# Attention and MLP-Mixer kernel on one core: laying older channel MLP steps between the token MLP's steps by their length

## The chip, the core and the metric

One core of one Trainium2 chip runs the whole program. The metric is the device time of one execution in microseconds (us). Times are told as the median of several runs, and one further execution is recorded by the hardware profiler; positions such as "at 455.01" are microseconds from the start of that recording's span.

TensorE (PE) multiplies into PSUM, of which this kernel gives each kind of product a few buffers. VectorE (DVE), ScalarE (ACT) and GpSimd (POOL) do the rest. SyncE (SP) issues most DMAs, ScalarE most loads of q and k. The program gives every engine its instructions in one fixed order.

## The reference

```python
scores = matmul(q, k.T) / 8                       # 8 batch rows, 8 heads, 576 tokens, 64 wide
scores = where(scores >= max(scores) - tau, scores, -1e9)
attn   = softmax(scores)
x      = (attn @ v) as (8, 576, 512)              # heads side by side
u      = x + (relu(x^T @ w_tok1) @ w_tok2)^T      # token MLP: 576 -> 256 -> 576
out    = u + relu(u @ w_ch1) @ w_ch2              # channel MLP: 512 -> 1536 -> 512
```

All of it is in 32-bit floats.

## The kernel before, in words

The kernel has one stream for attention and one for the two MLPs, and lays both into one order per engine by hand.

**Attention in units.** There are 144 units, 18 for each batch row b; unit u holds 128 query rows of a pair of heads. `scores(u)` (L290) makes the products `sc` on PE (L304), their maxima `mx` on VectorE (L309) and `bias` on GpSimd (L310). `weigh(u)` (L313) is ScalarE's: the threshold as a Prelu (L319, two instructions, which also set the two `sc` buffers free) and the exponential (L326, two). `norm` (L330) scales the result. Two units later `turn_blocks` (L359) turns it on VectorE (L367, tile `T`), and after every third unit 16 DMAs on SyncE's queue (L376) carry `T` into `eT`. I call these 16 an eT batch; there is one buffer for it. Two units after that, `values` (L393) multiplies `eT` by v on PE (tile `pv`, L411 and L416), and ScalarE copies the result to `xT` (L421).

**The token MLP.** When a row's last `values` is done, `push(b)` (L579) puts the row's token MLP in the list `todo`: five transposes `tx` (L447, each copied to `x_sb` by ScalarE, L448), two products `tok1` (L454, each with a Relu into `a` on ScalarE, L456), and eight products `tok2` (L464, each added to `xT` by VectorE, L468). The first `tok1` needs all five copies, the first `tok2` both Relus, and `xT` is what the channel MLP reads. So there are places where each step depends on the one just before it.

**The channel MLP.** Two batch rows are 1152 tokens, in groups i = 0 to 4 of 256 (the last of 128). Groups 0 and 1 come after the even row's token MLP, groups 2 to 4 after the odd one's. A group is 12 steps `ch1` (L501; four products each, L507, then a Relu on ScalarE, L508) and, for each 128 tokens, the steps `ch2` (L515; 12 products in all, L528, three to a step, then an addition or copy on VectorE, L540 or L546, and the output's DMA, L547). A product of 32-bit floats is two matmul instructions, so a `ch2` step of three products is six. From the second pair of rows on, `ch1(1)` also starts a turn of `xT` on VectorE (L491) and 16 DMAs on SyncE's queue (tile `ut`, L497), which are issued from `move_u` (L553). `tok1`, `tok2`, `ch1` and `ch2` share two PSUM buffers, tag `mm`; one `ch2` tile holds its buffer through all its steps.

**How the MLP's steps come into the order.** Each step in `todo` has an estimated cost in us. `push` sets a `quota` for each unit, such that some 45 us of steps (20 in the first row) are still left when the next row's token MLP arrives. In each unit `fill` (L566) takes steps until a share of the quota is used: 0.4 of it after the scores, before `weigh`, and three times 0.2 between the instructions of `weigh` (L322 to L328). The share in which a step falls decides where its ScalarE instruction stands: a Relu of the first share stands ahead of that unit's Prelus, one of the later shares behind them.

The steps left over (`old`) are the cover for the token MLP: `push` lays them between its steps (L588 to L591).

```python
for i, step in enumerate(steps):
    n = 2 if i in waits else 1
    todo.extend(old[:n] + [step])
    del old[:n]
```

Here `waits` holds two indices: that of the first `tok1` and that of the first `tok2`. So one old step stands ahead of each token step and two ahead of these, whatever the old steps' lengths are (`ch2` 2.6, `ch1` 1.72, in the group of 128 tokens 0.86). In this program `push(1)` finds 2 old steps of 2.6, the later rows find 19 to 23 steps of together 36 to 41.

Of the kernel before, what the change touches and what calls it, by code (L numbers as in the profile page):

```python
# [21 lines left out]
def kernel(  # L22
# [39 lines left out]
    NJ = DCH // P  # L62
# [162 lines left out]
    def weight(n):  # L225

        nonlocal steps_done
        for k in range(steps_done, min(steps_done + n, 3 * len(pieces) + 1)):
            i, part = divmod(k, 3)
            if part == 0:  # L230
                on_gpsimd(i - 1)
                if i:
                    load_piece(i - 1 + NRAW)
            else:
                on_scalar(i + 1, part - 1)
            on_vector(i, part)
            steps_done = k + 1
# [5 lines left out]
    def need(i):  # L243

        weight(3 * i + 4 - steps_done)
# [236 lines left out]
    def channel_mlp(b, uT, i):  # L482

        s = {}
        n = min(GR, 2 * S - GR * i)
        nt = n // P

        def turn_u():

            us, ut = s["us"], s["ut"]  # L490
            nc.vector.transpose(  # L491
                out=us[:, 0:nt].rearrange("q n a (c d) -> q c (n a) d", c=NCC),
                in_=uT[:, :, GR * i : GR * i + n].rearrange("q c (m r) -> q c m r", r=32),
            )

            def move(a, k):
                nc.sync.dma_start(out=ut[32 * a : 32 * a + 32, 0:nt, k, :], in_=us[32 * k : 32 * k + 32, 0:nt, a, :])  # L497

            moves.extend([lambda a=a, k=k: move(a, k) for a in range(4) for k in range(4)])

        def ch1(j):  # L501
            need(7 + j)
            if j == 0:
                s["g"] = work.tile([P, NJ, GR], F32, tag="g", bufs=1, name=f"g_{b}_{i}")
            ps = ps_mm.tile([P, GR], F32, tag="mm", name=f"c1_{b}_{i}_{j}")[:, 0:n]
            for c in range(NCC):
                nc.tensor.matmul(ps, lhsT=wc1[:, j, c, :], rhs=uT[:, c, GR * i : GR * i + n], start=(c == 0), stop=(c == NCC - 1))  # L507
            nc.scalar.activation(out=s["g"][:, j, 0:n], in_=ps, func=AF.Relu)  # L508
            if j == 1:
                s["us"] = work.tile([P, GR // P, 4, NCC * 32], F32, tag="us", bufs=1, name=f"us_{b}_{i}")  # L510
                if b:
                    s["ut"] = work.tile([P, GR // P, 4, NCC * 32], F32, tag="ut", bufs=1, name=f"ut_{b}_{i}")
                    turn_u()

        def ch2(t, part):  # L515
            need(7 + NJ + 3 * part + 2)
            t0 = GR * i + P * t
            if part == 0:
                s["ps"] = ps_mm.tile([P, NCC, P], F32, tag="mm", name=f"c2_{b}_{i}_{t}")
            ps = s["ps"]  # L520
            flat = ps.rearrange("q c d -> q (c d)")
            if part == 0 and not b:
                for c in range(NCC):
                    nc.tensor.matmul(
                        ps[:, c, :], lhsT=uT[:, c, t0 : t0 + P], rhs=ident, is_transpose=True, start=(c == 0), stop=False, skip_group_check=True
                    )
            for j in range(3 * part, 3 * part + 3):
                nc.tensor.matmul(  # L528
                    flat,
                    lhsT=s["g"][:, j, P * t : P * t + P],  # L530
                    rhs=wc2[:, j, :],
                    start=(j == 0 and b > 0),
                    stop=(j == NJ - 1),
                    skip_group_check=True,
                )
            if part == 3:
                o = s["us"][:, t].rearrange("q a x -> q (a x)")
                if b:
                    move_u()
                    nc.vector.tensor_add(  # L540
                        out=o.rearrange("q (c k d) -> q c k d", c=NCC, k=4),
                        in0=ps.rearrange("q c (k d) -> q c k d", k=4),
                        in1=s["ut"][:, t].rearrange("q k (c d) -> q c k d", c=NCC),
                    )
                else:
                    nc.vector.tensor_copy(out=o, in_=flat)  # L546
                nc.sync.dma_start(out=out[b : b + 2].rearrange("b s d -> (b s) d")[t0 : t0 + P, :], in_=o)  # L547

        return [(0.0067 * n, lambda j=j: ch1(j)) for j in range(NJ)] + [
            (2.6 if part or b else 3.0, lambda t=t, part=part: ch2(t, part)) for t in range(nt) for part in range(4)  # L550
        ]

    def move_u():  # L553
        while moves:
            moves.popleft()()
# [6 lines left out]
    todo = deque()  # L562
# [16 lines left out]
    def push(b):  # L579
        nonlocal quota  # L580
        uT = xTs[b]
        steps, waits = token_mlp(b) if b else token_mlp(b, range(NP // 2, NP))
        old = list(todo)
        todo.clear()
        todo.extend(early)
        early.clear()

        for i, step in enumerate(steps):  # L588
            n = 2 if i in waits else 1
            todo.extend(old[:n] + [step])  # L590
            del old[:n]  # L591
        todo.extend(old)
        for i in range(2) if b % 2 == 0 else range(2, (2 * S + GR - 1) // GR):
            todo.extend(channel_mlp(b - b % 2, uT, i))
        quota = (sum(c for c, _ in todo) - (KEEP if b else KEEP_FIRST)) / (UB - 1)
# [6 lines left out]
    def values_due(u):  # L602
        while due and due[0][0] <= u:
            _, b, p0, g = due.popleft()
            values(b, p0, g)
            if b == 0 and p0 == 0 and g == 2:
                return True
            if p0 == NP - 2 and g == 2:
                if not in_blocks(b):
                    return True  # L610
                push(b)
        return False

    for u in range(len(units) + LAG + 4):
# [4 lines left out]
        if on:  # L619
            b_now, p0, t = units[u]  # L620
            n = b_now * NP + p0
# [24 lines left out]
        if last and u < UB:  # L646
            early.extend(token_mlp(0, range(NP // 2))[0])
        elif last:
            push(0)
# [79 lines left out]
```

## Time and profile before

| | |
|---|---|
| median of 5 runs | 1353.02 us (1351.87 to 1355.48) |
| the profiled execution's own time | 1351.55 us |
| its span in the profile | 1349.8 us, 1.75 less than its time |
| mean granted clock of TensorE | 0.993 |
| `ch2` products (L528), 128x512 | 864 matmuls, 389.5 us busy |
| `ch1` products (L507) | 1920 matmuls, 399.6 us busy |
| `sc` products (L304) | 1280 matmuls, 192.9 us busy |
| eT batches (L376) | 672 DMAs, 108.0 KB each, median 2.3 us from issue to landing |

How to read it: the profile's "busy" of PE is a union of overlapping instructions, since matmuls are pipelined. What a product really takes is the distance from its start to the next one's start. In this profile that is 0.43 us for a matmul of 512 columns, 0.24 for `tok2`'s 288, 0.21 for 256 and 0.11 for 128, with hardly any spread; a longer distance is a wait. The first part of the run (to about 200 us) is short of MLP work and is not touched by the change.

### The profile page before, as it was taken

How to read it: one execution, taken by the hardware profiler on the slowest of the kernel's cores; microseconds unless marked ns; L12 is line 12 of the kernel's file. 1: busy time of each engine (PE TensorE's matmuls, PEld its weight loads, DVE VectorE, ACT ScalarE, POOL GpSimd, SP SyncE). 2: the span in 40 equal slices, each digit the busy share in tenths (PEclk: the TensorE clock that was granted, in tenths of full speed). 3: DMA queues.
4: the chain of work that ended last, by engine and by line, in shares of the span. 5: the costliest groups of instructions: out<-in, count | busy, mean ns of one | idle time of the engine just before them, and what ended most of it. 6: DMA issues, size and time to landing. Idle time of an engine off the chain costs nothing.

```text
span 1349.8 us, 17794 instructions
## 1 busy us (share of the span) xinstructions
PE 1303.3 (97%) x6138; PEld 808.8 (60%) x6138; DVE 592.6 (44%) x1024; ACT 585.3 (43%) x1299; POOL 353.6 (26%) x683
## 2 busy tenths in 40 slices
PE   6888899999999999999999999999999999999998
PEld 4555656547474666655665567565656566575675
DVE  6888874445443434444334445434433454201000
ACT  6777754445454435443434445353333444120110
POOL 4566652222222213221212222222221222100000
PEclk8998999999999999999999999999999999999999
DMA  5434774535353544543345435435443453400000
GB/s 123 118 90 124 203 174 95 129 93 131 91 136 80 119 103 100 128 103 90 85 110 128 95 88 126 116 82 119 106 103 84 118 112 82 115 16 18 22 24 32
DMA packets 296538, 135.31 MB, mean 100 GB/s; under 512 B 204736, under 2 KB 289216, under 8 KB 296448
## 3 DMA queue, kind: packets, MB, share of 16 engines
q1 hardware_dynamic: 167840, 118.15, 34.4%
q10 hardware_dynamic: 128608, 16.01, 7.5%
q8 instruction: 49, 0.80, 0.3%
q14 instruction: 41, 0.34, 0.1%
HBM read 43.25 MB, written 9.44 MB: 39 GB/s over the span
## 4 chain that ended last, share of the span: by engine, by line
PE 85%; DVE 6%; DMA 3%; ACT 2%; SPq 2%; POOL 1%; issue 1%; ACTq 0%; DVEq 0%; POOLq 0%
PE c L528 27%; PE c L507 25%; PE sc L304 11%; PE pv L416 8%; PE t L454 5%; PE t L464 4%; PE pv L411 3%; DVE mx L309 2%; SPq L376 2%; PE tx L447 1%; ACT e L319 1%; DMA eT<-T 1%; DMA lq<-in_q_dram 1%; DMA lk<-in_k_dram 1%; PE tr L355 1%
## 5 line engine op out<-in xcount | busy, mean ns | idle before, releaser
L309 DVE TENSOR_REDUCE mx<-sc 128x1 f32<-128x576 f32 x288 | 204.3, 750 | 445.9 <-PE sc L304 445.9
L507 PE MATMUL c<-xT,wc 128*128 128x256 f32 (+1 forms) x1920 | 399.6, 362 | 0.3 <-ACT g L508 0.3
L528 PE MATMUL c<-wc,g 128*128 128x512 f32 x864 | 389.5, 597 | 0.0
L507 PEld LDWEIGHTS c<-xT,wc 128*128 128x128 f32 x1920 | 334.4, 191 | 69.2 <-issue 29.3
L310 POOL TENSOR_SCALAR bias<-mx,toff 128x1 f32<-128x1 f32 x288 | 82.2, 285 | 774.2 <-DVE mx L309 719.2
L319 ACT ACTIVATE e<-sc,bias 128x576 f32<-128x576 f32 x288 | 199.2, 739 | 178.0 <-POOL bias L310 175.2
L528 PEld LDWEIGHTS c<-wc,g 128*128 128x128 f32 x864 | 159.2, 190 | 181.3 <-issue 177.9
L326 ACT ACTIVATE e<-e,ntau 128x576 f32<-128x576 f32 x288 | 221.1, 771 | 0.0
L337 POOL TENSOR_SCALAR e<-e,rr 128x576 f32<-128x576 f32 x288 | 214.4, 756 | 14.6 <-ACT g L508 2.6
L508 ACT ACTIVATE g<-c 128x256 f32<-128x256 f32 (+1 forms) x240 | 86.7, 361 | 294.1 <-PE c L507 275.9
L304 PE MATMUL sc<-kT,qT 64*128 64x288 f32 (+1 forms) x1280 | 192.9, 433 | 13.2 <-DVE kT L286 7.1
L367 DVE STREAM_TRANSPOSE T<-e 128x1152 f32<-128x1152 f32 x126 | 171.9, 1365 | 5.5 <-DMA eT<-T 3.5
L304 PEld LDWEIGHTS sc<-kT,qT 64*128 64x128 f32 (+1 forms) x1280 | 106.7, 178 | 99.7 <-issue 56.5
L416 PE MATMUL pv<-eT,lv 128*64 128x384 f32 (+1 forms) x1024 | 136.4, 406 | 0.0
L416 PEld LDWEIGHTS pv<-eT,lv 128*64 128x64 f32 x1024 | 76.3, 137 | 48.8 <-issue 40.1
L421 ACT COPY xT<-pv 128x384 f32<-128x384 f32 (+1 forms) x56 | 20.9, 400 | 165.9 <-PE pv L416 162.2
L540 DVE TENSOR_TENSOR us<-c,ut 128x512 f32<-128x512 f32 x27 | 18.6, 690 | 155.0 <-PE c L528 139.4
L464 PE MATMUL t<-w,a 128*128 128x288 f32 x256 | 75.2, 421 | 8.1 <-DVE xT L468 4.7
L454 PE MATMUL t<-x_sb,w 128*128 128x512 f32 (+1 forms) x180 | 72.4, 549 | 0.0
L464 PEld LDWEIGHTS t<-w,a 128*128 128x128 f32 x256 | 45.9, 192 | 30.1 <-issue 10.5
L468 DVE TENSOR_TENSOR xT<-xT,t 128x288 f32<-128x288 f32 x64 | 28.3, 446 | 71.0 <-PE t L464 70.5
L326 ACT ACTIVATION_READ_ACCUMULATOR e<-e,ntau 128x1 f32 x288 | 56.7, 197 | 0.0
(46 smaller groups left out, 542.9 us busy)
## 6 DMA issues: line engine op xcount, KB each, us to landing
eT<-T SPq DMA_DIRECT2D x672, 108.0 KB, 2.3
scratch<-in_moe_w_ch_dram SPq DMA_DIRECT2D x24, 512.0 KB, 3.7
lv<-in_v_dram SPq DMA_DIRECT2D x32, 288.0 KB, 3.2
out_dram<-us SPq DMA_DIRECT2D x36, 256.0 KB, 2.2
lk<-in_k_dram ACTq DMA_DIRECT2D x111, 72.0 KB, 2.6
lq<-in_q_dram ACTq DMA_DIRECT2D x106, 72.0 KB, 2.3
ut<-us SPq DMA_DIRECT2D x192, 32.0 KB, 1.9
lq<-in_q_dram SPq DMA_DIRECT2D x22, 72.0 KB, 3.3
```

Source lines behind the costliest of these rows:

```text
L304: nc.tensor.matmul(sc[h][rows, f, 0:HS], lhsT=qT[r, cols], rhs=kT[r, HS * f : HS * f + HS], start=True, stop=True)
L309: nc.vector.tensor_reduce(out=mx[:, c], in_=sc[h][:, :, 0:HS], axis=AX.XY, op=ALU.max)
L319: nc.scalar.activation(out=eh, in_=sc[h][:, :, 0:HS], func=AF.Prelu, bias=bias[:, h : h + 1], scale=SCALE, alpha=STEEP)
L326: nc.scalar.activation(out=eh, in_=eh, func=AF.Exp, bias=ntau, accum_out=rs[:, h : h + 1])
L337: nc.gpsimd.tensor_scalar(out=eh, in0=eh, scalar1=rr[:, h : h + 1], scalar2=1.0, op0=ALU.mult, op1=ALU.mult)
L367: nc.vector.transpose(out=T[:, :, place, :].rearrange("p a (c x) -> p c a x", c=NK), in_=e.rearrange("p (c a x) -> p c a x", c=NK, a=4))
L416: nc.tensor.matmul(to[r], lhsT=lv[:, j, :], rhs=e[j], start=False, stop=(c == NI - 1), skip_group_check=True)
L454: nc.tensor.matmul(to, lhsT=w1[:, t, P * m : P * m + P], rhs=x_sb[:, t, cols], start=(t == 0), stop=(t == NT - 1))
L464: nc.tensor.matmul(to, lhsT=a[:, m, P * c : P * c + P], rhs=w2[:, m, HS * f : HS * f + HS], start=(m == 0), stop=(m == NTK - 1))
L507: nc.tensor.matmul(ps, lhsT=wc1[:, j, c, :], rhs=uT[:, c, GR * i : GR * i + n], start=(c == 0), stop=(c == NCC - 1))
L508: nc.scalar.activation(out=s["g"][:, j, 0:n], in_=ps, func=AF.Relu)
L528: nc.tensor.matmul(flat, lhsT=s["g"][:, j, P * t : P * t + P], rhs=wc2[:, j, :], start=(j == 0 and b > 0), stop=(j == NJ - 1), skip_group_ ...
```

## The change

```diff
 def channel_mlp(b, uT, i):
+    J = 1 if b == 0 and i == 1 else 3
...
-        def ch2(t, part):
-            need(7 + NJ + 3 * part + 2)
+        def ch2(t, part, J):
+            need(7 + NJ + J * part + J - 1)
...
-            for j in range(3 * part, 3 * part + 3):
+            for j in range(J * part, J * part + J):
...
-            if part == 3:
+            if J * part + J == NJ:
...
-            (2.6 if part or b else 3.0, lambda t=t, part=part: ch2(t, part)) for t in range(nt) for part in range(4)
+            (0.867 * J + (0.0 if part or b else 0.4), lambda t=t, part=part: ch2(t, part, J)) for t in range(nt) for part in range(NJ // J)
         ]
...
     def push(b):
...
         for i, step in enumerate(steps):
-            n = 2 if i in waits else 1
-            todo.extend(old[:n] + [step])
-            del old[:n]
+            room = (3.4 if b == 1 else 5.0) if i in waits else 0.1
+            while old and room > 0:
+                room -= old[0][0]
+                todo.append(old.pop(0))
+            todo.append(step)
         todo.extend(old)
```

Ahead of a token step there is still one old step (a room of 0.1 is used up by any step). Ahead of the two steps in `waits` there are now as many as it takes to fill 5.0 us (3.4 for row 1). The `ch2` steps of group 1 of the first pair of rows, which are what `push(1)` finds, are cut to one product each, that is to two matmul instructions. The cost of a `ch2` step of three becomes 2.601 where it was 2.6. No instruction is added or removed: the change moves PE's steps, with the ScalarE, VectorE and SyncE instructions that belong to them, past the units' own instructions.

## Prediction, made before the changed kernel was run

> **What bounds the kernel now.** I read the busy shares first, then PE's waits, then the order of time around each of them, and at last the DMA queue of SyncE.
>
> ```profile
> PE 1303.3 (97%) x6138; PEld 808.8 (60%) x6138; DVE 592.6 (44%) x1024; ACT 585.3 (43%) x1299; POOL 353.6 (26%) x683
> ```
>
> PE is the bound, and the change neither adds nor removes one of its instructions. It can win only waits of PE, and lose only by new ones. PE's waits between 250 and 1180 us (engine, line, who was waited for: total us, times, longest) are few:
>
> ```profile
> PE t L464 <- ACT g L508: 3.2, 3, 1.6
> PE t L464 <- DVE xT L468: 1.8, 2, 1.3
> PE tx L447 <- ACT x_sb L448: 1.5, 2, 1.2
> PE pv L411 <- DMA lq<-in_q_dram: 0.5, 1, 0.5
> PE pv L411 <- DMA eT<-T: 0.3, 1, 0.3
> ```
>
> About 7 us, half of it the wait that the change aims at. Below I count from start to start, which gives 0.1 to 0.2 more for each. The releaser of the first is telling: not the Relu of `tok1` (L456) but one of `ch1` (L508). Around it, in unit 63:
>
> ```profile
> 450.21 1.24 PE L304 MATMUL sc<-kT,qT 64*128 64x288 f32 x8
> 451.38 2.05 PE L507 MATMUL c<-xT,wc 128*128 128x128 f32 x16
> 455.01 1.24 PE L464 MATMUL t<-w,a 128*128 128x288 f32 x4 [1.58 <-ACT g L508]
> ```
>
> Two short `ch1` fill both `mm` buffers. Their Relus stand behind the unit's Prelus on ScalarE, which wait for maxima and bias (452.63 to 454.04). The third user of a buffer waits, whoever it is.
>
> **A bound that is not in that list.** `values` needs its eT batch. From the turn `T` (L367) to the last landing it takes 12 to 15 us, and how much PE work lies between is set by the order. I took for each batch the landing (last issue plus some 2.3 us) and the start of `values`; the difference is its slack. From 200 us on it is under 1.2 us in twelve of 38 batches, and at the end of unit 36 PE waits already:
>
> ```profile
> 246.91 0.55 PE L411 MATMUL pv<-eT,vl 128*64 128x192 f32 x4 [1.70 <-DMA lq<-in_q_dram]
> ```
>
> (The load named is not what it waits for: in the built program this instruction waits for the batch, whose last DMA was issued by 244.0.) So each order that does less PE work between `T` and `values` pays there.
>
> **The change part by part.** I compared the orders in which the two built programs give PE its instructions, and counted at each unit and each `values` by how much more or less of the MLP stands ahead of it (0.86 us for a `ch2` product, 1.72 for a `ch1`, 0.86 for a short one, 0.97 for a `tok2`).
>
> *What goes.* (a) Row 1: seven single products now stand ahead of the transposes, one each, two ahead of `tok1`. The transposes waited 0.4 and 1.4 for ScalarE's copies (280.48, 282.38); with 0.86 between them, I find each copy (0.57) done in time: **-1.8**. (b) The first `tok2` waits 1.74, 0.99 and 0.99 in rows 2, 4, 6 (455.0, 770.4, 1086.9); as it comes later these go: **-3.7**. (c) Small waits of 0.24, three times, in row 4's `tok2` (779 to 794): -0.7. (d) `values` at 429.5 and 1088.3, which wait 0.3 and 0.4: -0.7. Together -6.9.
>
> *What takes its place on PE.* In row 2, unit 63, four short `ch1` stand where two stood. The third now needs the first one's buffer: ready at 454.04 + 0.26 = 454.3, wanted at 451.38 + 2 x 0.9 = 453.2, so 1.1, and 0.1 for the fourth: **+1.2**. In rows 4 and 6 the old steps go ahead of `tok1` so far that the first `tok1` slips behind the scores of units 98 and 134, into the first share of `fill`: its Relu then stands ahead of those units' Prelus, and the next scores, which need these buffers, wait. Before has this in unit 79, with a `ch1` of 1.72 as cover (order of time, all engines):
>
> ```profile
> 591.88 1.89 PE L507 MATMUL c<-xT,wc 128*128 128x256 f32 x8
> 592.08 0.60 ACT L456 ACTIVATE a<-t 128x512 f32<-128x512 f32 x1 [5.17 <-PE t L454]
> 592.57 1.36 ACT L319 ACTIVATE e<-sc,bias 128x576 f32<-128x576 f32 x2
> 593.70 1.53 PE L304 MATMUL sc<-kT,qT 64*128 64x288 f32 x8
> ```
>
> There the scores take 1.53 where others take 1.24: 0.3 lost. In units 98 and 134 the cover is 0.87, so 0.3 + 0.85, less what the first of the two buffers allows: 1.0 each, **+2.0** (bounds 0.3 and 1.2). Row 5 gets unit 79's pattern once, +0.3. In rows 4 and 6 no old step is left behind the last `tok2`: `ch1(0)` needs its buffer, which VectorE's addition frees some 2.2 after the scores' end (from 297.51 to 299.24 in unit 43, plus 0.45), while two `tok2` cover 1.94: 0.3 each, +0.7. Two or three `tok2` waits of the kind (c) arise in rows 2 and 6: +0.6. The `values` at 1088.3 still wait 0.3, with 0.1 of work put off: +0.4.
>
> *What the shifted order does to the batches.* (1) `values` of 246.9: one product (0.86) less ahead, batch unmoved, PE waits already: **+0.9**. (2) A whole `ch2` step (2.57) moves ahead of unit 52, so `T` comes 2.57 later against the work, and `values` at 383.71 stands where it stood:
>
> ```profile
> 363.25 1.24 PE L304 MATMUL sc<-kT,qT 64*128 64x288 f32 x8
> 364.42 5.42 PE L528 MATMUL c<-wc,g 128*128 128x512 f32 x12
> 369.77 1.24 PE L304 MATMUL sc<-kT,qT 64*128 64x288 f32 x8
> ...
> 383.71 0.55 PE L411 MATMUL pv<-eT,vl 128*64 128x192 f32 x4
> ```
>
> ```profile
> 367.57 13.47 SPq L376 DMA_DIRECT2D eT<-T  x16
> ```
>
> The batch ends at 381.04, its last DMA was issued 0.6 before and lands at 382.8: slack 0.9. Wait 2.57 - 0.9 = **+1.7** (0 if the batch shrinks to its shortest span, 10.3). (3) Unit 67 gets 2.57 more and a `tok2` (0.97) less ahead of it: 1.6 later, and its `T` 0.4 later still behind that `tok2`'s addition. From here SyncE's queue runs without a pause up to `values` at 530.56, which waits 0.45 already:
>
> ```profile
> 489.19 13.16 SPq L376 DMA_DIRECT2D eT<-T  x16
> 502.46 0.53 SPq L547 DMA_DIRECT2D out_dram<-us  x1
> 506.03 10.18 SPq L497 DMA_DIRECT2D ut<-us  x16
> 516.32 11.73 SPq L376 DMA_DIRECT2D eT<-T  x16
> ```
>
> (The gap at 503 is the output's landing, which VectorE's turn of `us` waits for.) The chain starts 2.0 later and `values` stands where it stood: **+2.0**. (4) The same chain from unit 103 (807.7) to `values` at 848.55: 2.2 less work between, slack 1.1, 0.3 of it won by the new wait above: +0.8. All other batches keep slack by the same count; the nearest is 0.7. In row 5 the 16 `ut` DMAs now stand ahead of one eT batch instead of behind it; that batch has 6.9 of slack.
>
> Sum of the new: 1.2 + 2.0 + 0.3 + 0.7 + 0.6 + 0.4 + 0.9 + 1.7 + 2.0 + 0.8 = 10.6. Against -6.9 that is **+3.7**, or 1355.2 beside the profiled execution's 1351.55 (span 1349.8 and 1.75 around it). That execution is at the lower end of the five runs; beside their median of 1353.02 it is 1356.7, and I say 1356.5.
>
> A rule that speaks against this: the Trainium skill, "DMA: Bandwidth & Descriptors", section on the anatomy of one DMA, gives a transfer about 2.0 us fixed plus bytes at 436 GB/s, and calls descriptor generation small. By it 16 transfers of 108 KB would be in place some 6 us after `T` (an estimate from that page, whose fit is for GpSimd's queue), every batch would have over 6 us of slack, and the sum would be -1.7. The trace differs: SyncE's queue takes 0.65 us for each issue, 10.3 for 16 and 13.5 where ScalarE issues loads meanwhile.
>
> **Rivals.** *The batches are not late.* Where ScalarE issues no loads within a batch, the batch takes 10.3 and not 13.2 to 13.5. The loads stand behind ScalarE's exponentials, which move too. If they drop out of batches (1) to (4), each lands some 3 us sooner: the 5.4 of new waits vanish and with them the 0.45 at 530.6. That gives 3.7 - 5.9 = -2.2: 1350.8. It decides from 2.6 us per batch on. For it: batches of 12 us exist. Against it: the loads hang on the same units as `T`, so they move along. *Half and half:* batches (1) and (3) wait since they wait already, (2) and (4) do not, and the scores in units 98 and 134 wait 0.3: 3.7 - 2.5 - 1.4, about 0: 1353. *Worse:* a late `values` also delays the next batch, since there is one `eT` buffer; two further batches with 1 us of slack fail by 2 each: 1361. *The change does little:* in rows 3 and 7 it moves only one or two steps, and their `tok2` do not wait in the profile; that is in the sum as nothing.
>
> **How the numbers follow.** The forecast has 0.48, the first rival 0.27, half and half 0.20, worse 0.05. A measurement of this kernel can tell 0.2%, 2.7 us, from no change. The forecast lies 1 us beyond that, so I put 0.43 of its 0.48 to slower and 0.05 to the same; with worse, slower has 0.48. The first rival (1350.8) lies just inside the bound: 0.13 faster, 0.14 the same. Half and half: 0.17 the same, 0.03 faster. So 0.16, 0.36, 0.48. The range takes in the forecast with its bounds (scores 0.3 to 1.2, batch (2) from 0) and most of the first rival: 1349.5 to 1361.
>
> **What would show it.** Right: the waits of `t` for `g` give way to one of a `ch1` in unit 63; scores wait for L319 in units 99 and 135; `values` near 247, 384, 531 and 849 wait 2.6, 1.7, 2.4 and 0.8. Wrong: these `values` start without a wait, or the last DMA of their batches lands under 12 us behind `T`.

## The result, and the profile after

The changed kernel takes **1357.82 us** (median, 1353.43 to 1361.11), the one before 1354.64 us beside it (1350.22 to 1357.71): ratio **1.0024, 95% interval 1.0019 to 1.0029**, 3.2 us more. A second series gave 1.0023 (1.0010 to 1.0036). Single executions of one kernel lie up to 10 us apart. In the two profiled executions the first 200 us, whose program the change does not touch, differ by 3.6 to 4.0 us; the places where the granted clock is 0.5 in the first 150 us differ too, but whether the one comes of the other is not shown. I therefore compare the profiles from the first maximum of unit 36 (at 240.31 before, 244.35 after) to the end: 1109.5 us before, 1112.0 after, **+2.5**; the second profile of the changed kernel has +3.9.

Lines behind `ch1` have moved by 3 or 4: L507, L508, L497, L528 are now L510, L511, L500, L532. The page's busy times after:

```profile
PE 1311.4 (97%) x6138; PEld 814.2 (60%) x6138; DVE 593.3 (44%) x1024; ACT 584.7 (43%) x1299; POOL 353.5 (26%) x683
```

PE has the same 6138 instructions and 8.1 us more of busy time. A wait is not busy time, so not only waits have come: some products take longer, in part in those first 150 us. PE's waits after, 245 to 1190 us (total us, times, longest):

```profile
PE pv L411 <- DMA lq<-in_q_dram: 3.1, 3, 2.2
PE t L464 <- DVE xT L468: 1.8, 2, 1.3
PE pv L411 <- DMA eT<-T: 1.7, 2, 1.2
PE sc L304 <- ACT e L319: 0.9, 2, 0.4
PE c L510 <- ACT g L511: 0.8, 1, 0.8
```

In this list `t` no longer waits for `g`, and `tx` no longer for `x_sb`: what the change aimed at is gone. In its place stand `values` (L411) that wait for DMAs, two scores that wait for L319, and one `ch1`. (For the load named first, `lq`, the prediction's caution holds: `values` needs the batch.) That `ch1` is the third short one of unit 63, in the order of time:

```profile
456.71 2.05 PE L510 MATMUL c<-xT,wc 128*128 128x128 f32 x16
...
459.26 0.27 ACT L511 ACTIVATE g<-c 128x128 f32<-128x128 f32 x1
...
459.59 2.08 PE L510 MATMUL c<-xT,wc 128*128 128x128 f32 x16 [0.82 <-ACT g L511]
```

The wait of 1.74 (start to start) has become one of 0.99, of the same Relu, one instruction further on. The scores of unit 99 wait for `e`, which stands behind `tok1`'s Relu (L456) on ScalarE:

```profile
769.49 0.60 ACT L456 ACTIVATE a<-t 128x512 f32<-128x512 f32 x1 [5.38 <-PE t L454]
769.98 1.36 ACT L319 ACTIVATE e<-sc,bias 128x576 f32<-128x576 f32 x2
...
770.77 1.87 PE L304 MATMUL sc<-kT,qT 64*128 64x288 f32 x8 [0.43 <-ACT e L319]
...
772.57 2.84 PE L454 MATMUL t<-x_sb,w 128*128 128x512 f32 x6
```

They start 0.50 late (start to start), and from their start to the next product 1.80 go by, where it is 1.17 elsewhere: they wait a second time in their course, for the second of the two buffers. Together 1.1, and the same in unit 135.

And the `values` of unit 54. Its batch runs 12.97 where it ran 13.47, and starts nearer to it:

```profile
374.47 12.97 SPq L376 DMA_DIRECT2D eT<-T  x16
```

```profile
389.34 0.55 PE L411 MATMUL pv<-eT,vl 128*64 128x192 f32 x4 [1.23 <-DMA eT<-T]
```

**What the prediction had not counted on** stands behind the wait of unit 36:

```profile
250.57 0.55 PE L411 MATMUL pv<-eT,vl 128*64 128x192 f32 x4 [2.17 <-DMA lq<-in_q_dram]
250.92 1.97 PE L416 MATMUL pv<-eT,lv 128*64 128x192 f32 x16
```

The same 16 products take 1.50 elsewhere, and the second half of this `values` (253.25) takes 2.48. From the end of the wait to the next scores 5.1 us go by; two such halves elsewhere take 3.4. The stretch around it (us, PE, PEld, DVE, ACT, POOL busy, then the granted clock, DMA share, GB/s):

```profile
252.00:256.00 4.00, 4.00 (x29) 3.46 (x26) 0.00 (x0) 0.24 (x2) 0.00 (x0) 0.60 0.03 6
```

The granted clock is 0.60 on the mean of these 4 us, 1.00 in those behind them; in the kernel before it is 1.00 throughout at this place. In the records it is 0.5 from 251.8 to 255.2, for 3.41 us; the other steps down within the run are as long, or twice or three times as long. It costs 1.7.

Counted as in the prediction (time shift of each `values` and unit, less the shift of the work ahead of it), the profiled difference falls into: unit 36 +0.5, clock +1.7, `tx` -1.9, `values` at 389 +1.3, at 429 -0.3, row 2 -0.4, `values` at 536 +0.05, at 753 +0.5, row 4 -0.4, scores of unit 106 (at 829.75) +0.4, row 5 +0.3, row 6 +0.8. Sum +2.5. The scores of unit 106 take 1.54 where others take 1.17; ahead of them VectorE's turn of `us` (L494, from 826.39, 1.25 long) stands in front of the maxima, which the Prelus that free their buffers need. `values` at 851.47 do not wait.

### The profile page after: what moved, and what is told of

The parts are those of the page before. It is cut to its first block, busy times and chain, and to the rows that moved or that the text cites. A ratio compares the mean times of both kernels' runs of the same rounds, so it can differ in the third digit from the quotient of the medians.

```text
span 1356.3 us, 17809 instructions
## 1 busy us (share of the span) xinstructions
PE 1311.4 (97%) x6138; PEld 814.2 (60%) x6138; DVE 593.3 (44%) x1024; ACT 584.7 (43%) x1299; POOL 353.5 (26%) x683
## 4 chain that ended last, share of the span: by engine, by line
PE 85%; DVE 5%; DMA 3%; ACT 3%; SPq 1%; issue 1%; POOL 1%; ACTq 0%; DVEq 0%; POOLq 0%
PE c L532 27%; PE c L510 25%; PE sc L304 11%; PE pv L416 9%; PE t L454 5%; PE t L464 4%; PE pv L411 3%; DVE mx L309 2%; SPq L376 1%; ACT e L319 1%; PE tx L447 1%; DMA lk<-in_k_dram 1%; DMA lq<-in_q_dram 1%; PE tr L355 1%; ACT e L326 1%
## 5 line engine op out<-in xcount | busy, mean ns | idle before, releaser
L510 PE MATMUL c<-xT,wc 128*128 128x256 f32 (+1 forms) x1920 | 398.3, 362 | 1.3 <-ACT g L511 1.3
L532 PE MATMUL c<-wc,g 128*128 128x512 f32 x864 | 390.3, 597 | 0.0
L510 PEld LDWEIGHTS c<-xT,wc 128*128 128x128 f32 x1920 | 333.7, 191 | 69.5 <-issue 27.8
L310 POOL TENSOR_SCALAR bias<-mx,toff 128x1 f32<-128x1 f32 x288 | 82.1, 285 | 779.9 <-DVE mx L309 723.1
L319 ACT ACTIVATE e<-sc,bias 128x576 f32<-128x576 f32 x288 | 199.0, 739 | 176.0 <-POOL bias L310 172.3
L532 PEld LDWEIGHTS c<-wc,g 128*128 128x128 f32 x864 | 159.7, 190 | 175.6 <-issue 171.1
L511 ACT ACTIVATE g<-c 128x256 f32<-128x256 f32 (+1 forms) x240 | 86.7, 361 | 292.8 <-PE c L510 280.8
L304 PE MATMUL sc<-kT,qT 64*128 64x288 f32 (+1 forms) x1280 | 196.2, 440 | 13.5 <-DVE kT L286 8.6
```

The source lines that it names most:

```text
L304: nc.tensor.matmul(sc[h][rows, f, 0:HS], lhsT=qT[r, cols], rhs=kT[r, HS * f : HS * f + HS], start=True, stop=True)
L319: nc.scalar.activation(out=eh, in_=sc[h][:, :, 0:HS], func=AF.Prelu, bias=bias[:, h : h + 1], scale=SCALE, alpha=STEEP)
L532: nc.tensor.matmul(flat, lhsT=s["g"][:, j, P * t : P * t + P], rhs=wc2[:, j, :], start=(j == 0 and b > 0), stop=(j == NJ - 1), skip_group_ ...
```

## The experiments

The last column is the profile's time from unit 36 to the end, as a difference to before's. It is of one execution, the ratio of 6 to 46. In microseconds, 0.001 of a ratio is 1.35.

| run | what it is | ratio to before (95%) | us | from unit 36 |
|---|---|---|---|---|
| after | the change | 1.0024 (1.0019 to 1.0029) | +3.2 | +2.5 |
| after_again | the change once more | 1.0023 (1.0010 to 1.0036) | +3.1 | +3.9 |
| cut_only | row 1 cut, old laying | 1.0001 (0.9991 to 1.0010) | +0.1 | +2.1 |
| lay_only | new laying, no cut | 1.0015 (1.0004 to 1.0025) | +2.0 | +3.8 |
| lay_not3 | new laying but in row 3, no cut | 1.0000 (0.9988 to 1.0011) | 0.0 | -0.1 |
| cut_kept | one tile of row 1 cut, later units unmoved | 0.9987 (0.9979 to 0.9996) | -1.8 | -1.3 |
| cut_kept_lay24 | the same, new laying in rows 2 and 4 | 0.9970 (0.9958 to 0.9981) | -4.1 | -2.7 |
| after_lay24 | the change, new laying in rows 2 and 4 alone | 1.0000 (0.9989 to 1.0012) | 0.0 | +1.3 |
| lay_second | the change, old laying ahead of `tok1` | 1.0008 (0.9998 to 1.0018) | +1.1 | +3.1 |
| fill_wait | the change, two products in unit 36's wait | 1.0017 (1.0005 to 1.0029) | +2.3 | +3.0 |
| after_pool | the change, GpSimd issues q and k | 1.0006 (0.9996 to 1.0016) | +0.8 | -3.3 |
| before_pool | before, GpSimd issues q and k | 0.9996 (0.9984 to 1.0007) | -0.5 | -2.7 |
| best_pool | cut_kept_lay24, GpSimd issues q and k | 0.9991 (0.9980 to 1.0002) | -1.2 | -5.3 |

My theory A when I began: the cut moves work past batches whose length is fixed, and that is the loss; the laying by length gains a little. The rival B: the laying is the loss, and the cut is harmless.

**1. The cut alone.** The changed kernel with the old rule in `push`:

```diff
-            room = (3.4 if b == 1 else 5.0) if i in waits else 0.1
-            while old and room > 0:
-                room -= old[0][0]
-                todo.append(old.pop(0))
-            todo.append(step)
+            n = 2 if i in waits else 1
+            todo.extend(old[:n] + [step])
+            del old[:n]
```

> The cut of row 1's channel steps to single products, with the old rule (one old step, two ahead of the first tok1 and tok2) in every row. Theory A: the cut is what costs. It takes one product (0.86 us) from ahead of the values at the end of unit 36 and puts a step of 2.57 ahead of unit 52, so the values near 250 wait 2.2 (1.7 before), those near 387 wait 1.3, and TensorE's clock falls to half for one stretch of 3.4 us after the wait near 250 (1.7 lost); the transposes' waits of 1.8 go. Sum about +1 to +2.5 us against before. Theory B (the laying by length costs, the cut only helps): -1.8 us, no new waits of values.

Measured +0.1 (-1.2 to +1.4): between the two theories. The `tx` waits are gone, `values` of units 36, 54 and 96 wait 3.42, 1.32 and 0.56, and the clock is at 0.5 for 3.4 us behind the first. The profiled execution was the slowest of twelve, so a wait of 3.42 is not this kernel's rule. By its time the cut alone brings about as much as it costs.

**2. The laying alone.** `J = 3` in place of `J = 1 if b == 0 and i == 1 else 3`.

> The laying by length in all rows, row 1's channel steps left at three products. Theory A: about 0 (-1 to +1 us against before): the waits of the first tok2 (1.74, 0.99, 0.99) go or shrink, the scores of units 99 and 135 wait 0.5 each, unit 116's 0.3; unit 36's values wait 1.7 as before and the clock stays whole after them; unit 54's values start without a wait. Theory B: +2 to +3.5 us, nearly all that the change costs.

Measured +2.0: nearer to B. But the profile puts it in one place that neither theory had. In row 3 the second `tok1` now stands right ahead of the scores of unit 80, without a `ch1` between:

```profile
593.79 4.46 PE L454 MATMUL t<-x_sb,w 128*128 128x512 f32 x10
...
598.29 0.60 ACT L456 ACTIVATE a<-t 128x512 f32<-128x512 f32 x1 [3.91 <-PE t L454]
...
599.57 1.87 PE L304 MATMUL sc<-kT,qT 64*128 64x288 f32 x8 [1.32 <-ACT e L319]
```

The Prelus of unit 79 stand behind `tok1`'s Relu, and the scores wait for them, 1.39 from start to start; in their course they lose another 0.6, as in unit 99. And from 601.6 to 605.1 the clock is at 0.5, as behind the wait of unit 36:

```profile
602.00:606.00 4.00, 4.00 (x13) 3.21 (x13) 2.05 (x4) 0.38 (x1) 1.92 (x4) 0.62 0.72 171
```

Row 3 costs 3.4 more there than in the kernel before. So the same with the old rule in row 3:

```diff
+            if b == 3:
+                n = 2 if i in waits else 1
+                todo.extend(old[:n] + [step])
+                del old[:n]
+                continue
             room = (3.4 if b == 1 else 5.0) if i in waits else 0.1
```

> The kernel with the new laying and no cut in row 1 (+2.0 us in the runs above), with the old laying in row 3 alone. Theory A, row 3 is what cost it: the wait of 1.39 us for tok1's Relu in unit 80 and the clock window of 0.5 behind it (3.4 us together in its profile) go: -1.4 us on before (ratio 0.999), between -2 and -0.5. Theory B, that wait and window belong to one execution, and the laying costs by its order in every row: +2.0 still (1.0015).

Measured 0.0 (-1.6 to +1.5): the 2 us are gone, and the wait and the clock step with them (row 3's stretch, units 72 to 90, takes 164.4 where it took 168.5). A's -1.4 lies inside the interval, B's +2.0 outside. In the change itself a `ch1` (1.82 from start to start) stands between that `tok1` and the scores of unit 80, which lose 0.3 as in the kernel before: cut and laying do not simply add up.

**3. The gains alone.** In `cut_kept` only the second tile of that group is cut, and the filler holds back 0.867 (one product) more in row 1, so that from row 2 on every step but one `ch1` near unit 78 stands as before. The list of `ch2` steps calls `cut(t)` in place of `J`:

```diff
-        J = 1 if b == 0 and i == 1 else 3
+        def cut(t):
+            return 1 if b == 0 and i == 1 and t == 1 else 3
...
-        quota = (sum(c for c, _ in todo) - (KEEP if b else KEEP_FIRST)) / (UB - 1)
+        quota = (sum(c for c, _ in todo) - (KEEP + 0.867 if b == 1 else KEEP if b else KEEP_FIRST)) / (UB - 1)
```

> Only the second tile's steps of group 1 are cut to single products, the old rule in every row, and the amount kept back in row 1 is raised by the one product that is left over more, so that all later units get the same steps as before (by the order of the instructions, only units 40, 41 and 78 have other work ahead of them). Theory A: the transposes' waits go and nothing else comes: -1.8 us against before (-1.2 to -2.3). If the gain of the cut is given back somewhere that is neither the batches nor the clock, it is 0.

Measured -1.8. A product now stands between the transposes, which start without a wait:

```profile
281.21 0.66 PE L447 MATMUL tx<-ident,xT 128*128 128x128 f32 x4
281.70 1.02 PE L531 MATMUL c<-wc,g 128*128 128x512 f32 x2
282.57 0.60 PE L447 MATMUL tx<-ident,xT 128*64 128x128 f32 x4
```

With the laying by length (5.0) in rows 2 and 4 on top of it:

> As cut_kept, and the laying by length (5.0) in rows 2 and 4 alone, where the traces show it to win. Theory A: a further -0.4 (row 2) and -0.4 (row 4, whose scores of unit 99 wait 0.5): -2.6 us against before, -0.2%. Theory B: worse than cut_kept by 1 us or more.

Measured -4.1 (-5.7 to -2.6), from six runs: **faster than both kernels**; A's -2.6 is the edge of the interval. Its profile has row 2 at -0.3 and row 4 at -0.7; no clock step, and unit 36 waits 1.37. From unit 36 on it is only 1.4 below that of cut_kept, and half of this is a batch: `values` of unit 72 wait 0.69 there and not here. The waits of 1.74 and 0.99 that the laying was meant to cover are both still there, now of a `ch1`; what goes in row 4 are two of 0.24. So what the laying adds to the cut in time (2.3) is not explained by what it covers.

**4. The clock.** Two products that nobody needs fill part of unit 36's wait:

```diff
+            if (b, p0, g, i) == (1, 2, 1, SHARES[g][0][0]):
+                for _ in range(2):
+                    nc.tensor.matmul(whole, lhsT=ident, rhs=wc2[:, 0, :], start=True, stop=True, skip_group_check=True)
```

> The changed kernel with two needless products (128x512, 0.86 us each, thrown away) ahead of the values of unit 36, where its profile shows PE waiting 2.24 us and, right after, one 3.4-us window at a granted clock of 0.5. Theory A, the shorter idle time keeps the clock up: the wait falls to about 0.5, no window at 0.5 near 250 us, and the products behind it take 3.2 us again instead of 4.8: 1.7 less than the changed kernel (+3.2 on before), so +1.5 us on before (ratio 1.0011), although PE does 1.7 us more work. Theory B, the window has nothing to do with that wait: the two products go into the idle time, so +3.2 (1.0024), and the window at 0.5 is still there. If the wait was not idle time at all, +4.9 (1.0036).

The profile does what A says. The needless products, then the wait, then `values` at full speed:

```profile
245.24 1.88 PE L411 MATMUL pv<-wc,ident 128*128 128x512 f32 x4
247.84 0.55 PE L414 MATMUL pv<-eT,vl 128*64 128x192 f32 x4 [0.73 <-DMA eT<-T]
248.19 1.50 PE L419 MATMUL pv<-eT,lv 128*64 128x192 f32 x16
```

There is no step to 0.5 near it, and units 36 to 45 take 69.0 where the changed kernel takes 70.4, with 1.7 us more of work in them. This is one execution. The time, +2.3 (+0.7 to +3.9), does not tell A's +1.5 from B's +3.2: that execution lost 2.0 elsewhere, in unit 72, whose `values` waited 2.5 (the recorded expectations call this unit 75; by its maxima the place, 530.56 before and 535.56 after, lies in unit 72). Hence the changed kernel once more:

> The changed kernel once more, unchanged, for a second profile of the same order. In the runs so far values of unit 75 waited 0.6 us in the changed kernel and 2.5 in the same order with two products more in unit 36, and unit 36 itself waited from nothing to 3.4 us where the order up to it was the same. Theory A, how ScalarE's issues fall between SyncE's decides it in each execution: these two waits come out at other values than 2.24 and 0.58 (by more than 0.5 in one of them), the waits that no batch sets (0.99 in unit 63, 0.50 in units 99 and 135) come out the same within 0.05, and the time is +3.2 on before as it was (ratio 1.0024). Theory B, the order sets them: all within 0.1 of the first profile.

Units 36, 54, 72 and 96 wait 2.39, 1.86, 1.21 and 0.62 (2.24, 1.30, 0.58, 0.45 in the first profile); the waits that no batch sets are 0.99, 0.50 and 0.50, as they were. A's mark was a difference of over 0.5 in one of units 36 and 72: unit 72 has 0.63. The five profiles with the whole cut and ScalarE's loads (fill_wait apart) side by side:

| run | wait in unit 36 | clock step behind it | wait in unit 72 |
|---|---|---|---|
| after | 2.24 | yes | 0.58 |
| after_again | 2.39 | yes | 1.21 |
| lay_second | 2.67 | yes | 1.71 |
| cut_only | 3.42 | yes | 0.33 |
| after_lay24 | 1.86 | no | 1.63 |

In the five whose order up to unit 36 is the old one (before, lay_only, lay_not3, cut_kept, cut_kept_lay24) it waits 1.77, 1.62, 1.44, 1.48 and 1.37, never with the step. How much of the wait lies within one step of 3.41 us matters: counted on the grid of these steps, PE is idle for at most 2.17, 2.32, 2.37 and 2.25 in one of them in the four cases with a step down, for 1.79 in after_lay24, and before's 1.77 is split into 1.17 and 0.52. The Trainium skill, "TensorE: Matmul & The Clock Gate", Part 1 (the HAM clock gate), has the clock go to half after at least one idle window of 3.4 us, windows that run free. The grid and the half agree with the trace; that the window must be idle throughout, as one may read it, does not: 2.2 is enough here. And in unit 80 of lay_only 1.32 were enough, while fill_wait's wait in unit 72 has 1.83 in one step and no step down behind it. Ahead of unit 36, where PE has less to do, steps down stand behind 1.1 to 2.9 of idle time in one step, and up to 1.7 passed without one. So idle time alone does not decide it; what else does stays open.

**5. The batches.** The loads of q and k that stretch them go to GpSimd's queue:

```diff
-                    load_qk(n + m, (nc.scalar if b_now else nc.sync,) * 2, range(lo, hi))
+                    load_qk(n + m, (nc.gpsimd if b_now else nc.sync,) * 2, range(lo, hi))
```

> The changed kernel with the q and k loads of the later rows issued by GpSimd and not by ScalarE. Theory A, these issues are what stretches SyncE's batches of 16 from 9.7 to as much as 13.0 us, and the batches are what the changed kernel waits for: every batch takes about 9.7 to 10, the waits of values in units 36, 54, 75, 96 and later (2.2, 1.3, 0.6, 0.4, 0.4, 0.6) and the clock window (1.7) go, about -7 on the changed kernel, so 1351 where before is 1354.6 (ratio 0.997). Theory B, the issues of two engines disturb each other whichever they are: batches as long as now, the changed kernel's time, +3.2 (1.0024). Theory C, GpSimd's own work waits behind its issues and takes the gain back: over 1358 (above 1.0024), with new waits of PE for POOL.

A's half on the batches came true. The second batch of the chain ahead of unit 72:

```profile
517.24 10.27 SPq L376 DMA_DIRECT2D eT<-T  x16
```

No `values` from unit 54 on waits 0.3 any more, unit 36 waits 1.40 without a clock step, and from unit 36 to the end the kernel takes 5.8 less than the changed kernel's first profile, close to A's 7. But the time is only 2.4 less, and the profiled execution was the fastest of the twelve, 3.7 below their median. One cost of the edit is C's: GpSimd also computes the Prelus' bias (L310). Where loads are issued three in a row (around 190 us), that bias stands behind them, and the scores wait 0.74 for it. The clearest case is in best_pool:

```profile
192.76 0.70 POOL L105 DMA_DIRECT2D lk<-in_k_dram  x1
193.45 0.67 POOL L105 DMA_DIRECT2D lq<-in_q_dram  x1
194.11 0.67 POOL L105 DMA_DIRECT2D lk<-in_k_dram  x1
...
194.81 0.49 POOL L310 TENSOR_SCALAR bias<-mx,toff 128x1 f32<-128x1 f32 x2
...
195.91 1.86 PE L304 MATMUL sc<-kT,qT 64*128 64x288 f32 x8 [1.97 <-ACT e L319]
```

Three issues of 0.67 to 0.70, and the scores wait 1.97. All three profiles with this edit also have a step of the clock at 164, which none of the others has there. Whether these two make up the rest of the time is not shown. In both kernels the same edit, so that no batch but unit 36's is late in either (1.40 after, 0.69 before):

> The kernel before with the q and k loads of the later rows issued by GpSimd. Theory A: batches of 9.7 to 10 us, the waits of values (1.8, 0.5, 0.3, 0.3, 0.4) go, about -3 on before (ratio 0.998); with the changed kernel in the same form at +0.8 on before in its run, the change would still be a loss of 3 to 4 without a single late batch, so the batches could not be its main cost. Theory B, the batches are the main cost of the change: then this kernel stands at most 1 us under the changed kernel in the same form, -0.2 or more (ratio 0.9998 or above).

Measured -0.5 (-2.2 to +0.9): A's -3 lies outside, B's mark of -0.2 inside. after_pool had +0.8: 1.3 apart (each to within about 1.5), where with the late batches the kernels are 3.2 apart. The two times alone do not exclude 3.2. By the profiles, one of each, from unit 36 on, after_pool is 0.6 *below* before_pool, where the changed kernel is 2.5 to 3.9 above the one before. So B fits better: late batches, and the clock step behind one of them, are the main cost of the change by the profiles; without them it would be about even.

> The version that stood at -4.1 us on before (one tile of row 1 cut, the later units kept where they were, the new laying in rows 2 and 4 alone), with the q and k loads of the later rows issued by GpSimd as well. Theory A, what is late there are batches (its profile shows waits of values of 0.4 and 0.5, and unit 36 can wait up to 2): these go, and it stands at -5 to -6 (ratio 0.9955 to 0.9963). Theory B, GpSimd's additions now wait behind its issues and cost what the batches give: -4.1 or less of a gain (0.997 or above).

Measured -1.2 (-2.7 to +0.3): B. The part from unit 36 on is the best of all (-5.3), and units 27 to 36 take 66.4 in place of 62.7.

**6. Which part of the laying.** The old rule in all rows but 2 and 4 (`if b not in (2, 4):` ahead of the same lines as in lay_not3):

> The changed kernel with the old laying (two steps, then one each) in rows 1, 3, 5, 6 and 7, and the new one in rows 2 and 4 alone; row 1's steps are cut as in the changed kernel. Theory A, the new laying wins 0.3 and 0.7 in rows 2 and 4 and costs 0.3 and 0.8 in rows 5 and 6: 1.1 under the changed kernel, so +2.1 on before (ratio 1.0016). Theory B, all the loss is the cut's: the same as the changed kernel, +3.2 (1.0024). Theory C, the laying is the loss wherever it is made: only rows 2 and 4 are left of it, so under +1 (1.0007 or less).

Measured 0.0 (-1.5 to +1.6): below A's +2.1, as C has it. Yet what its profile lacks against the changed kernel is mainly the clock step (unit 36 waited 1.86 in it), though the two programs are the same up to that unit. Whether rows 3, 5, 6 and 7 of the laying cost 1 us or 3 is not settled by it.

The old rule ahead of the first `tok1` alone:

```diff
-            room = (3.4 if b == 1 else 5.0) if i in waits else 0.1
+            room = 5.0 if i == waits[1] else 0.1
+            if i == waits[0]:
+                todo.extend(old[:2])
+                del old[:2]
+                room = 0.0
```

> The changed kernel (row 1 cut) with the older steps laid two ahead of the first tok1, as before the change, and 5.0 us of them ahead of the first tok2 alone. The first tok1 of rows 4 and 6 then stands ahead of the scores of units 98 and 134 again. Theory A, tok1's Relu ahead of those units' exponentials is what held the next scores: their waits for L319 (0.50 in units 99 and 135) go, and the first tok2 still does not wait: about 1 us under the changed kernel, so +2.2 on before (ratio 1.0016). Theory B, the scores wait because PE comes to them earlier: 0.5 still, or a wait of a first tok2 of 0.5 or more in their place, the changed kernel's time (1.0024).

Measured +1.1 (-0.3 to +2.4): A's +2.2 lies inside, B's +3.2 outside. The scores of units 99 and 135 do not wait for L319 any more: the mechanism is right. But the second half of B is right too. In their place the `ch1` behind two short ones waits, as in unit 63:

```profile
777.57 1.16 PE L510 MATMUL c<-xT,wc 128*128 128x128 f32 x8 [0.82 <-ACT g L511]
```

It is 0.99 in unit 99 and again in row 6, and from unit 36 on the profile is no shorter than the changed kernel's. The time is; by which part stays open.

## Why the prediction was right, and where not

The forecast was +3.7 on the one execution, measured are +3.2 (2.6 to 3.9): the side and the size are right, and so is the main reason, `values` that come to wait for batches. That the sum is so close is in part luck: several terms erred, with opposite signs.

- **(a) the transposes, -1.8:** -1.9 in the profile, -1.8 alone (cut_kept). Right.
- **(b) and unit 63, -1.74 + 1.2:** -1.74 + 0.99, the releaser as foretold. The first `tok2` of rows 4 and 6 wait no more. Right.
- **Scores behind `tok1`'s Relu, 1.0 each in units 99 and 135:** place and releaser right (lay_second takes them away). The start is 0.50 late, and 0.62 more go in their course, 1.1 each: the size is right too. Row 5's +0.3 came in unit 116, whose scores take 1.46 for 1.17. With the 0.99 of unit 63 the laying hands back some 3.2 of the 3.7 under (b).
- **Batch (1), +0.9:** +0.5 and +0.6 in two profiles. Over the two times five profiles of part 4 unit 36 waits 2.5 with the cut and 1.5 without it on average: +1.0. Right.
- **Batch (2), +1.7:** 1.30, 1.86, 1.55, 1.50 and 1.32 in the five. Right.
- **Batch (3), +2.0: the step that failed.** "The chain starts 2.0 later and `values` stands where it stood" took the queue's lengths as given. The chain is, after:

```profile
512.44 10.19 SPq L500 DMA_DIRECT2D ut<-us  x16
522.74 10.48 SPq L376 DMA_DIRECT2D eT<-T  x16
```

  The last batch takes 10.48 where it took 11.73, the first 12.73 where it took 13.16. That gives back 1.7 of the 2.0: `values` waits 0.58 where it waited 0.52. In after_again the two batches give back nearly as much (1.6), but from the first issue of the second to its last landing it is 12.9 and not 12.5 (13.9 before), and `values` waits 1.21. In the four other profiles of the table in part 4 it waits 0.33 to 1.71, so the term is about +0.6 on average (mean 1.09), and varies; fill_wait had 2.5. The prediction knew that a batch may shrink, but in its rivals, where it let (1) to (4) shrink together or (2) and (4) alone.
- **Batch (4), +0.8: wrong place.** `values` at 851 do not wait in the profile. 0.4 is lost earlier, in the scores of unit 106: that the turn of `us` on VectorE can hold up the maxima was not in the count.
- **"All other batches keep slack": wrong.** Unit 96 waits 0.45 to 0.62 in all profiles with the whole cut and ScalarE's loads and not before; its last DMA lands 14.5 behind its first issue instead of 12.4.
- **Missing: the clock, +1.7.** I summed waits as if the products behind them cost nothing more. It came in four of the five profiles of that table, and nearly replaces what (3) lacked: that is the luck.
- **The first rival** (no late batches, -2.2) was made by hand: after_pool against before_pool, -0.6 by the profiles, from unit 36 on, where the rival had -2.2. It is not what happens with ScalarE's loads in place.

## What to carry to other kernels

When a scheduler moves work of an engine that is 97% busy, the gains are the few waits it covers, and the price is paid at every transfer whose slack was the work moved away: list the slack of all of them first, and change the order only where nothing late stands behind (cut_kept: -1.8 with one of the two ideas that together cost +3.2; with both of them, in rows 2 and 4 alone, -4.1 in time and -2.7 in the profile). A wait of PE over 2 us may cost almost twice its length by the clock step behind it (2.24 and 1.7 in unit 36), so split long waits with work, or keep them short. And a DMA queue's time per transfer is not a constant: here it depended on who else issues. Moving those issues to another engine has a price there, in what stands behind them.

## What the runs showed of the hardware

- From unit 36 on, the granted clock fell to 0.5 for one step of 3.41 us behind idle times of 2.17 to 2.37 us within one step, and 1.32 us in one other place, not behind 1.79 or less at the first place, nor behind 1.83 in unit 72 of fill_wait; each step cost 1.7 us.
- SyncE takes about 0.65 us for each of these issues when it is alone (10.3 for an eT batch). From unit 36 on a batch takes 10.3 to 13.7 when ScalarE issues two to six loads meanwhile, and 10.3 to 11.6 when GpSimd issues them. The number of loads alone does not set it: the last batch of the chain has five in both kernels and takes 11.73 before, 10.48 after. GpSimd takes 0.67 to 0.70 for each, on the engine itself.
- Waits that an engine sets came out equal in every profile of one order (0.99, 0.50); waits that a batch sets differed by up to 0.63 us between two executions of the same program.
